# Attention products with V written three half-heads behind their scores, in a fused attention and mixer kernel

## The chip, the cores and the metric

The kernel runs on one core of one Trainium2 chip. The metric is the device time of one execution in microseconds, the median of several runs. Before the change it is 428.05 us, the median of 3 runs from 427.13 to 430.08.

## The reference, cut to what matters

Two batches of 12 heads, 448 tokens, head size 64: causal attention, then a mixer over tokens and channels, then a gated mixer. Only the attention part and what takes its output are touched by the change.

```python
scores = where(causal_mask, -1e9, q @ k.T / 8)
attn   = exp(scores - rowmax(scores)); attn = attn / (rowsum(attn) + 1e-9)
x      = attn @ v                                   # batch 2, heads 12, 448 x 64
h      = relu(x.T @ w_tok1) @ w_tok2;  u = x + h.T  # mix over tokens
y      = u + relu(u @ w_ch1) @ w_ch2                # mix over channels
# then gelu(y @ w_in), layer norm, a product over tokens, gate, w_out, residual
```

## The kernel before, in words

Heads are taken in **pairs** (12 pairs over both batches), and each head in two **halves**, so there are 48 half-heads. A half takes two of the four blocks of query rows (`HALVES`, `KW`), so that every half has 512 columns of scores at most. For one half-head, `probabilities` (lines 268 to 305) does this:

- TensorE: scores `s_ps` from q and k in f32 (line 286), into one of 2 PSUM buffers.
- VectorE: mask and row minimum into `pe` (line 291; 5 buffers, and 2 of their own for the first half of a second head).
- ScalarE: the bias (296), the exponential (298), the f16 high part `hl` (300; 4 buffers).
- GpSimd: the f16 low part of `hl` (301).
- SP: a transposing DMA from `hl` to `pT` (303; `pT` has 4 buffers).

`values` (316 to 328) then multiplies the transposed probabilities with V: three f16 products for each block of keys (lines 326, 327, 328). A pair has 60 of them, 20 on each line, and 18 records of score matmuls on line 286; over the 12 pairs that is 720 and 216. They gather in `x_ps`, of which there is one PSUM buffer, so that the first product of a pair waits until the pair before has been normalised out of it (342 to 344).

`prep_v` (248) loads V of one pair, finds its largest value, and splits it into f16 parts `vh` and `vl`, of which there are two sets that alternate by pair. `prep_qk` (239) loads q and k. `prepare` calls `prep_qk` four heads ahead and `prepare_v` calls `prep_v` two heads ahead; the latter stands in `tc.high_priority(offset=-80)`, which moves its instructions back in the order by 80 places. `load_tok` (233) brings in the weights of the token mix, each through ScalarE, VectorE and GpSimd. After every fourth head `token_mix` (356) multiplies the normalised `xh`, `xl` into `a_ps` and `u_ps`. `channel_up` (170) for seven of the column blocks of batch 0 can run beside attention: its weight loads stand in SP's queue behind the transposes of given heads (`issue_after(marks[...])`).

**What sets the order.** The program text is not the order in the queues. A planner runs the program against its own estimates of durations and gives each engine, at each moment, the instruction that is ready by these estimates (operands done, buffer free) and was written first. The result is a fixed queue for each engine, and on the chip each engine takes its queue in that order. Writing an instruction later therefore only means that others win against it when both are ready.

Of the kernel before, what the change touches and what calls it, by code (L numbers as in the profile page):

```python
# [11 lines left out]
F32 = mybir.dt.float32  # L12
# [15 lines left out]
def mixer_kernel(  # L28
# [20 lines left out]
    H, D = 2 * H2, D2 // 2  # L49
# [3 lines left out]
    P = 128  # L53
# [3 lines left out]
    GH = 4  # L57
# [1 line left out]
    WC = 768  # L59
    NF0 = 7  # L60
    AHEAD = 4
    VAHEAD = 2

    def f32(ap):
        return ap.bitcast(F32)
# [130 lines left out]
    with ExitStack() as at:  # L196
# [7 lines left out]
        ps_x = at.enter_context(tc.tile_pool(name="ps_x", bufs=1, space=PSUM))  # L204
# [28 lines left out]
        def load_tok():  # L233
            for c in range(NQ):
                load64(w1h[:, c, :], w1l[:, c, :], w_tok1[tok(c), :], "pool", twice=c == 0)
            for c in range(NT):
                load64(w2h[:, c, :], w2l[:, c, :], w_tok2[c * P:(c + 1) * P, :], "pool")
# [10 lines left out]
        def prep_v(b, n):  # L248

            vr = qkp.tile([P, NVC, 2 * D], F32, tag="vr", name="vr", bufs=2)  # L250
            nc.sync.dma_start(vr, v[b, n])
            hi, lo = vts[n % NVT]
            vr4 = vr.rearrange("p c (h d) -> p c h d", h=2)
            am = stp.tile([P, 1], BF16, tag="am", name="am")
            nc.vector.tensor_reduce(am, vr[:, 1:5], AX.XY, ALU.max, apply_absolute_value=True)
            pm = ps_e.tile([P, 512], F32, tag="d", name="vm")
            nc.tensor.matmul(pm[:, :P], am.to_broadcast([P, P]), ident_b, start=True, stop=True)
            sv = stp.tile([P, 1], F32, tag="sv", name="sv")
            nc.vector.reduce_max(sv, pm[:, :P], axis=AX.X)
            nc.vector.tensor_scalar(sv, sv, 1e-20, 1.0 / VSCALE, ALU.max, ALU.mult)  # L260
            nc.vector.reciprocal(sv, sv)
            nc.scalar.activation(hi[:, :, :, :D], vr4, AF.Copy, scale=sv[:, 0:1])
            nc.vector.scalar_tensor_tensor(lo, vr4, sv[:, 0:1], hi[:, :, :, :D], ALU.mult, ALU.subtract)
            return hi, lo, sv

        count = [0]

        def probabilities(qp, k2, hd, half):

            ps = ps_s.tile([P, NP], F32, tag="s", name="s_ps")
            if (hd, half) == (1, 0):
                pe, mx = pes[count[0] % len(pes)], mxs[count[0] % len(pes)]
            else:
                pe = xp.tile([P, NP], F32, tag="pe", name="pe", bufs=NPE)
                mx = stp.tile([P, 2], F32, tag="mx", name="mx")
            todo, o = [], 0
            for j, i in enumerate(HALVES[half]):
                w = KW[i]  # L280
                if i > 0 or hd == 0:
                    todo.append((j, i, slice(o, o + w)))
                    q0 = S - 64 if i == 0 else S + w - P if hd else w - P - 64
                    for ks in KEYS[i]:
                        m = ks.stop - ks.start
                        nc.tensor.matmul(ps[:, o:o + m], qp[:, q0:q0 + P], k2[:, ks], start=True, stop=True)  # L286
                        o += m
                else:
                    o += w
            for j, i, cs in todo:  # L290
                nc.vector.tensor_tensor_reduce(  # L291
                    out=pe[:, cs], in0=ps[:, cs], in1=mask0 if i == 0 else mask[:, MASKS[i]],
                    scale=-1.0 / math.sqrt(D), scalar=3.0e38, op0=ALU.add, op1=ALU.min, accum_out=mx[:, j:j + 1],
                )
            bias = stp.tile([P, 2], F32, tag="bias", name="bias")
            nc.scalar.add(bias, mx, math.log(PSCALE))
            for j, i, cs in todo:
                nc.scalar.activation(pe[:, cs], pe[:, cs], AF.Exp, bias=bias[:, j:j + 1], scale=-1.0)  # L298
            hl = hlp.tile([P, 2, NP], F16, tag="hl", name="hl", bufs=4)
            nc.scalar.copy(hl[:, 0], pe)  # L300
            nc.gpsimd.tensor_sub(hl[:, 1], pe, hl[:, 0])  # L301
            pT = hlp.tile([P, 2, NP // P, P], F16, tag="pT", name="pT", bufs=4)
            last[0] = nc.sync.dma_start_transpose(
                out=pT.rearrange("p a c q -> p (a c) q"), in_=hl.rearrange("p a n -> p (a n)")
            ).ins
            return pT
# [9 lines left out]
        def values(px, pT, hd, half, vh, vl):  # L316


            for i in HALVES[half]:
                for h in range(2) if i == 0 and hd == 0 else [hd] if i else []:  # L320
                    n = 64 if i == 0 else P
                    qs = slice(h * 64, h * 64 + 64) if i == 0 else slice(0, P)
                    o = px[qs, 2 * i - 1 + h if i else 0]
                    for j, (blk, c) in enumerate(MEET[i]):
                        ph, pl = pT[:, 0, blk, qs], pT[:, 1, blk, qs]
                        nc.tensor.matmul(o, ph, vh[:, c, h, :D + 1], start=j == 0, stop=False)  # L326
                        nc.tensor.matmul(o[:, :D], ph, vl[:, c, h, :], start=False, stop=False, skip_group_check=True)
                        nc.tensor.matmul(o, pl, vh[:, c, h, :D + 1], start=False, stop=j == i)

        def pair(b, e, qk, vs, x):  # L330

            (vh, vl, sv), (xf, xh, xl) = vs, x
            px = ps_x.tile([P, 7, D + 1], F32, tag="x", name="x_ps")
            for hd in range(2):
                for half in range(2):
                    pT = probabilities(*qk, hd, half)
                    values(px, pT, hd, half, vh, vl)
                if hd == 0:
                    yield
            count[0] += 1  # L340
            rd = stp.tile([P, 7, 1], F32, tag="rd", name="rd")
            nc.vector.tensor_scalar(rd, px[:, :, D:D + 1], 1e-9 * PSCALE, sv[:, 0:1], ALU.add, ALU.mult)
            nc.vector.reciprocal(rd, rd)
            nc.vector.tensor_mul(xf[:, e], px[:, :, :D], rd.to_broadcast([P, 7, D]))
            cs = slice(e * P, (e + 1) * P)
            x6 = xf[:, e, 1:].rearrange("p (c h) d -> p c (h d)", h=2)
            nc.scalar.copy(xh[:, 1:, cs], x6)
            sub(xl[:, :, cs], x6, xh[:, 1:, cs])

            for h in range(2):  # L350
                hs, ls = (slice(64 * i, 64 * i + 64) for i in (h, 1 - h))
                ds = slice(e * P + h * D, e * P + h * D + D)
                nc.gpsimd.tensor_scalar(xh[hs, 0, ds], xf[hs, e, 0], 1.0, 0.0, ALU.mult, ALU.add)
                sub(xh[ls, 0, ds], xf[hs, e, 0], xh[hs, 0, ds])
# [37 lines left out]
        last, marks = [None], []  # L392
        order = [(b, h) for b in range(B) for h in range(H)]
        qks, vss = {}, {}

        def prepare(n):
            if n < len(order):
                b, h = order[n]
                if h % 2 == 0:
                    qks[b, h // 2] = prep_qk(b, h // 2)  # L400

        def prepare_v(n):
            if n < len(order) and n % 2 == 0:
                b, h = order[n]

                with tc.high_priority(offset=-80):
                    vss[b, h // 2] = prep_v(b, h // 2)
# [3 lines left out]
        def up():  # L411

            m = dense.pop(0)
            with tc.issue_after(marks[H - 2 + m]):
                channel_up(m, [0], rpool, ps_e)

        for n in range(AHEAD):
            prepare(n)
        for n in range(VAHEAD):
            prepare_v(n)  # L420
        for n, (b, h) in enumerate(order):
            prepare(n + AHEAD)
            prepare_v(n + VAHEAD)
            if n == GH - 1:
                load_tok()
            if h % GH == 0:
                x = (
                    xp.tile([P, GH // 2, 7, D], F32, tag="xf", name="xf", bufs=2),
                    xp.tile([P, NQ, GH * D], F32R, tag="xh", name="xh"),
                    xp.tile([P, NQ - 1, GH * D], F32R, tag="xl", name="xl"),  # L430
                )
            if h % 2 == 0:
                it = pair(b, h % GH // 2, qks[b, h // 2], vss[b, h // 2], x)
            next(it, None)
            marks.append(last[0])
            if h % GH == GH - 1:
                token_mix(b, h // GH, *x)

            if (b, h) == (1, H - 2):
                up()  # L440

        while dense:
            up()
# [175 lines left out]
```

## Time and profile before

| what | value |
|---|---|
| median of 3 runs | 428.05 us (427.13 to 430.08) |
| the profiled execution | 429.13 us, span 427.3 us from its first to its last instruction |
| mean granted TensorE clock | 0.988 of full |
| busy share of the span | PE 94%, PEld 80%, POOL 58%, DVE 56%, ACT 48% |
| scores run | 4.6 to 141.7 us |
| products with V run | 18.4 to 154.3 us |

PE is TensorE's matmuls, PEld its weight loads, DVE VectorE, ACT ScalarE, POOL GpSimd, SPq the queue of SP, which issues the DMAs. A row of a table by stretches gives, for each engine, busy us and in brackets the number of its instructions, then the mean granted clock, the mean busy share of the 16 DMA engines and what they moved. A row of a timeline gives start, duration, engine, line, operation, tiles, the count of merged instructions, and in square brackets how long the engine sat idle before and what released it.

### The profile page before, as it was taken

The page shows a single profiled execution, that of the slowest core. Times are in us where ns is not written, and L with a number is a line of the kernel's source. Part 1 is how long each engine was busy: PE and PEld are TensorE (multiplying, and loading weights), DVE is VectorE, ACT ScalarE, POOL GpSimd, SP SyncE. Part 2 cuts the span into 40 slices and gives each one's busy share as a digit, 9 for nine tenths or more (in the row PEclk, how much of TensorE's full clock was granted, in tenths as well). Part 3 has the DMA queues.
Part 4 walks back from the last instruction along what each step waited for, and adds up shares of the span by engine and source line. Part 5 has one row for each costly group of instructions (what it writes and reads, how often), then busy time and mean ns, then how long its engine had stood idle before and what let it go on. Part 6 is the DMA issues. An engine that isn't in the chain of part 4 may idle for free.

```text
span 427.3 us, 6998 instructions
## 1 busy us (share of the span) xinstructions
PE 399.9 (94%) x2567; PEld 340.3 (80%) x2567; DVE 238.4 (56%) x522; ACT 204.2 (48%) x389; POOL 246.5 (58%) x234
## 2 busy tenths in 40 slices
PE   5878788888998999999999999999999999999996
PEld 3545666776787998999999999999998889965995
DVE  5989566787693645344444275557437451249422
ACT  3888678697665454445344244334423232332100
POOL 2789768769777564464335247454556653225662
PEclk9989999999898999999999999999999999999999
DMA  7999999999987854446344344453354001100122
GB/s 213 199 290 235 209 173 208 252 220 265 242 170 164 163 160 154 137 156 220 123 132 157 106 127 144 134 181 110 126 163 135 0 0 51 49 2 0 76 98 86
DMA packets 66738, 62.29 MB, mean 146 GB/s; under 512 B 53136, under 2 KB 58384, under 8 KB 66704
## 3 DMA queue, kind: packets, MB, share of 16 engines
q1 hardware_dynamic: 66704, 61.85, 56.5%
q8 instruction: 20, 0.33, 0.3%
q14 instruction: 14, 0.11, 0.1%
HBM read 46.50 MB, written 2.75 MB: 115 GB/s over the span
## 4 chain that ended last, share of the span: by engine, by line
PE 67%; DMA 12%; POOL 8%; ACT 5%; SPq 2%; issue 2%; DVE 2%; POOLq 0%; ACTq 0%; DVEq 0%
DMA pT<-hl 8%; PE y_ps L137 7%; PE y_ps L136 7%; PE y_ps L138 7%; PE r_ps L138 6%; PE r_ps L136 6%; PE r_ps L137 6%; POOL hl L301 4%; DMA vr<-in 2%; PE v_ps L138 2%; PE o_ps L136 2%; PE o_ps L138 2%; PE o_ps L137 2%; PE ug_ps L136 2%; PE v_ps L137 2%; PE ug_ps L138 2%
## 5 line engine op out<-in xcount | busy, mean ns | idle before, releaser
L94 POOL TENSOR_TENSOR wlo<-wm,whi 128x768 fp32r<-128x768 f32 (+1 forms) x41 | 81.3, 1984 | 75.6 <-ACT whi L121 75.1
L116 DVE TENSOR_SCALAR wm<-wm 128x768 int32<-128x768 int32 (+2 forms) x53 | 34.1, 643 | 88.0 <-ACT wm L113 88.0
L301 POOL TENSOR_TENSOR hl<-pe,hl 128x512 f16<-128x512 f32 x48 | 60.5, 1267 | 29.2 <-ACT hl L300 25.2
L113 ACT ACTIVATE wm<-wraw 128x768 f32<-128x768 f32 (+2 forms) x53 | 42.7, 805 | 59.1 <-POOL wlo L94 47.7
L286 PE MATMUL s_ps<-k,q 128*128 128x64 f32 (+3 forms) x216 | 57.9, 410 | 8.3 <-DMA q<-in 4.6
L138 PE MATMUL r_ps<-u_hi,wlo 128*128 128x448 f32 x144 | 53.4, 370 | 0.0
L137 PE MATMUL r_ps<-u_lo,whi 128*128 128x448 f32 x144 | 53.2, 369 | 0.0
L136 PE MATMUL r_ps<-u_hi,whi 128*128 128x448 f32 x144 | 53.1, 369 | 0.0
L136 PE MATMUL y_ps<-rh,whi 128*128 128x448 f32 x144 | 52.6, 365 | 0.0
L138 PE MATMUL y_ps<-rh,wlo 128*128 128x448 f32 x144 | 52.6, 365 | 0.0
L137 PE MATMUL y_ps<-rl,whi 128*128 128x448 f32 x144 | 52.6, 365 | 0.0
L121 ACT CAST whi<-wm 128x768 fp32r<-128x768 f32 (+1 forms) x41 | 32.8, 800 | 37.8 <-PE ug_ps L137 11.6
L117 DVE SCALAR_TENSOR_TENSOR wm<-wraw,wm 128x768 int32<-128x768 int32 (+2 forms) x53 | 50.1, 945 | 1.0
L286 PEld LDWEIGHTS s_ps<-k,q 128*128 128x128 f32 x216 | 32.4, 208 | 17.2 <-issue 6.6
L298 ACT ACTIVATE pe<-pe,bias 128x192 f32<-128x192 f32 (+3 forms) x84 | 40.2, 522 | 0.4
L291 DVE CUSTOM_DVE_ANT_0 pe<-s_ps,mask 128x320 f32<-128x320 f32 (+3 forms) x84 | 34.6, 444 | 7.9 <-PE s_ps L286 6.1
L300 ACT CAST hl<-pe 128x512 f16<-128x512 f32 x48 | 29.3, 612 | 18.3 <-DMA pT<-hl 17.9
L326 PE MATMUL x_ps<-vh,pT 128*128 128x65 f16 (+1 forms) x240 | 26.3, 197 | 11.6 <-DMA pT<-hl 10.9
L326 PEld LDWEIGHTS <-pT 128*128 128x128 f16 (+1 forms) x240 | 21.2, 98 | 19.6 <-DMA pT<-hl 14.6
L94 POOL TENSOR_TENSOR u_lo<-yt,u_hi 128x448 fp32r<-128x448 f32 x12 | 13.9, 1156 | 30.1 <-ACT u_hi L193 30.1
L138 PEld LDWEIGHTS r_ps<-u_hi,wlo 128*128 128x128 f32 x144 | 27.2, 189 | 2.6 <-issue 0.4
L136 PEld LDWEIGHTS r_ps<-u_hi,whi 128*128 128x128 f32 x144 | 27.3, 189 | 2.4 <-issue 0.2
(140 smaller groups left out, 918.7 us busy)
## 6 DMA issues: line engine op xcount, KB each, us to landing
wraw<-in SPq DMA_DIRECT2D x35, 768.0 KB, 4.5
wraw<-in SPq DMA_DIRECT2D x14, 512.0 KB, 3.9
vr<-in SPq DMA_DIRECT2D x12, 320.0 KB, 3.8
k<-in SPq DMA_DIRECT2D x12, 224.0 KB, 3.4
q<-in SPq DMA_DIRECT2D x24, 112.0 KB, 3.4
out<-ob SPq DMA_DIRECT2D x12, 224.0 KB, 1.9
wraw<-in SPq DMA_DIRECT2D x3, 256.0 KB, 3.1
pT<-hl SPq DMA_TRANSPOSE x48, 4.4
```

The lines of the kernel that those rows point to most:

```text
L94: nc.gpsimd.tensor_sub(lo, src, f32(hi))
L113: nc.scalar.activation(m, words.bitcast(F32)[:, :, 1], AF.Prelu, scale=2.0 ** -112, alpha=-(2.0 ** 32))
L116: nc.vector.tensor_scalar(mi, mi, 3, None, ALU.logical_shift_left)
L117: nc.vector.scalar_tensor_tensor(mi, words[:, :, 0], 29, mi, ALU.logical_shift_right, ALU.bitwise_or)
L136: nc.tensor.matmul(ps, lh, rh, start=i == 0 and not begun, stop=False)
L137: nc.tensor.matmul(ps, lh, rl, start=False, stop=False)
L138: nc.tensor.matmul(ps, ll, rh, start=False, stop=i == n - 1)
L286: nc.tensor.matmul(ps[:, o:o + m], qp[:, q0:q0 + P], k2[:, ks], start=True, stop=True)
L291: nc.vector.tensor_tensor_reduce(out=pe[:, cs], in0=ps[:, cs], in1=mask0 if i == 0 else mask[:, MASKS[i]], scale=-1.0 / math.sqrt(D), scal ...
L298: nc.scalar.activation(pe[:, cs], pe[:, cs], AF.Exp, bias=bias[:, j:j + 1], scale=-1.0)
L301: nc.gpsimd.tensor_sub(hl[:, 1], pe, hl[:, 0])
L326: nc.tensor.matmul(o, ph, vh[:, c, h, :D + 1], start=j == 0, stop=False)
```

## The change

Each half-head's `probabilities` is put on a list, and `products()`, which does the `values` of the oldest entry, is called once the list holds more than `LAG = 3`. So the products of a half-head are written behind the scores, exponentials and transposes of the three half-heads that follow it, also across heads and pairs. The normalisation of a pair, the next V preparation and the token mix move with the products. V of the first pair is prepared right behind q and k of the first pair and without the offset of 80; V of a later pair is prepared behind the normalisation of the pair two before it. No arithmetic, tile size or buffer count changes.

```diff
-    VAHEAD = 2
+    LAG = 3
...
-        def pair(b, e, qk, vs, x):
-
-            (vh, vl, sv), (xf, xh, xl) = vs, x
-            px = ps_x.tile([P, 7, D + 1], F32, tag="x", name="x_ps")
-            for hd in range(2):
-                for half in range(2):
-                    pT = probabilities(*qk, hd, half)
-                    values(px, pT, hd, half, vh, vl)
-                if hd == 0:
-                    yield
-            count[0] += 1
+        def normalise(px, e, sv, x):
+            xf, xh, xl = x
             rd = stp.tile([P, 7, 1], F32, tag="rd", name="rd")
...
         def prepare_v(n):
-            if n < len(order) and n % 2 == 0:
+            if n < len(order):
                 b, h = order[n]
                 with tc.high_priority(offset=-80):
                     vss[b, h // 2] = prep_v(b, h // 2)
...
-        for n in range(AHEAD):
-            prepare(n)
-        for n in range(VAHEAD):
-            prepare_v(n)
-        for n, (b, h) in enumerate(order):
-            prepare(n + AHEAD)
-            prepare_v(n + VAHEAD)
+        waiting = []
+        px = x = None
+        def products():
+            nonlocal px, x
+            b, h, half, pT = waiting.pop(0)
+            vh, vl, sv = vss[b, h // 2]
+            if (h % 2, half) == (0, 0):
+                px = ps_x.tile([P, 7, D + 1], F32, tag="x", name="x_ps")
+            values(px, pT, h % 2, half, vh, vl)
+            if (h % 2, half) != (1, 1):
+                return
...
+            normalise(px, h % GH // 2, sv, x)
+            prepare_v(b * H + h + 3)
+            if h % GH == GH - 1:
+                token_mix(b, h // GH, *x)
+
+        prepare(0)
+        vss[0, 0] = prep_v(0, 0)
+        for n in range(1, AHEAD):
+            prepare(n)
+        prepare_v(2)
+        for n, (b, h) in enumerate(order):
+            prepare(n + AHEAD)
             if n == GH - 1:
                 load_tok()
...
-            if h % 2 == 0:
-                it = pair(b, h % GH // 2, qks[b, h // 2], vss[b, h // 2], x)
-            next(it, None)
+            for half in range(2):
+                waiting.append((b, h, half, probabilities(*qks[b, h // 2], h % 2, half)))
+                if len(waiting) > LAG:
+                    products()
+            count[0] += h % 2
             marks.append(last[0])
-            if h % GH == GH - 1:
-                token_mix(b, h // GH, *x)
             if (b, h) == (1, H - 2):
                 up()
+        while waiting:
+            products()
         while dense:
             up()
```

## Rows read from the trace of the kernel before

**Rows 1.** By stretches: length; PE, PEld, DVE, ACT, POOL busy; clock, DMA, GB/s.

```profile
0.00:140.00 140.00, 116.84 (x1119) 90.02 (x1120) 100.93 (x313) 102.11 (x233) 104.58 (x128) 0.96 1.00 217
140.00:170.00 30.00, 29.31 (x213) 26.51 (x213) 16.04 (x30) 15.49 (x26) 17.05 (x16) 1.00 0.63 166
...
180.00:420.00 240.00, 240.00 (x1172) 211.44 (x1171) 116.77 (x173) 82.92 (x125) 120.31 (x88) 1.00 0.33 105
...
20.00:50.00 30.00, 22.99 (x264) 16.57 (x265) 25.26 (x82) 24.39 (x62) 27.04 (x32) 0.94 1.12 246
...
200.00:220.00 20.00, 20.00 (x101) 18.53 (x100) 8.79 (x14) 8.98 (x14) 8.68 (x5) 1.00 0.49 149
```

**Rows 2.** The chain that ended last, by engine and by line.

```profile
PE 67%; DMA 12%; POOL 8%; ACT 5%; SPq 2%; issue 2%; DVE 2%; POOLq 0%; ACTq 0%; DVEq 0%
```

**Rows 3.** Waits of the engines: us in total, times, longest.

```profile
ACT hl L300 <- DMA pT<-hl: 17.9, 11, 4.6
...
PE x_ps L326 <- DMA pT<-hl: 10.9, 11, 2.3
...
DVE am L255 <- DMA vr<-in: 9.7, 8, 3.5
```

**Rows 4.** Instructions of tile pT: DMA to landing.

```profile
DMA to landing us min/median/max: 3.0/4.4/7.3
```

**Rows 5.** By stretches, the score matmuls of line 286 alone.

```profile
0.00:26.70 26.70, 15.84 (x54) 9.14 (x54) 1.00 0.91 215
...
0.00:80.20 80.20, 41.09 (x150) 23.12 (x150) 0.98 1.04 216
```

**Rows 6.** By stretches, the products with V of line 326 alone.

```profile
0.00:26.70 26.70, 2.40 (x20) 1.82 (x20) 1.00 0.91 215
...
0.00:80.20 80.20, 13.40 (x120) 10.72 (x120) 0.98 1.04 216
```

**Rows 7.** By stretches, the low parts on GpSimd (line 301) alone.

```profile
0.00:80.20 80.20, 38.27 (x31) 0.98 1.04 216
```

**Rows 8.** Timeline of GpSimd around the first and the sixth pair's normalisation.

```profile
24.81 0.56 POOL L353 TENSOR_SCALAR xh<-xf 64x64 fp32r<-64x64 f32 x2 [0.78 <-DVE xf L344]
...
26.13 1.16 POOL L301 TENSOR_TENSOR hl<-pe,hl 128x512 f16<-128x512 f32 x1
...
82.04 1.15 POOL L353 TENSOR_SCALAR xh<-xf 64x64 fp32r<-64x64 f32 x4
```

**Rows 9.** Timelines of the start: SP, DVE, ACT and PE.

```profile
3.02 1.10 SPq L245 DMA_DIRECT2D q<-in  x2
...
5.94 1.06 SPq L251 DMA_DIRECT2D vr<-in  x2
...
10.92 1.35 SPq L303 DMA_TRANSPOSE pT<-hl  x1
...
10.03 0.69 DVE L255 TENSOR_REDUCE am<-vr 128x1 bf16<-128x512 f32 x1 [0.48 <-DMA vr<-in]
...
18.20 1.10 DVE L263 SCALAR_TENSOR_TENSOR vl<-vr,sv,vh 128x640 f16<-128x640 f32 x1
...
17.30 1.53 ACT L262 ACTIVATE vh<-vr,sv 128x640 f16<-128x640 f32 x2
...
11.45 1.19 PE L286 MATMUL s_ps<-k,q 128*128 128x64 f32 x4
...
18.38 0.22 PE L326 MATMUL x_ps<-vh,pT 128*64 128x65 f16 x1
```

**Rows 10.** Waits of SP's queue: us in total, times, longest.

```profile
SPq L303 <- PE x_ps L328: 8.3, 6, 5.0
```

**Rows 11.** Timelines around 75 to 90 us: GpSimd and SP.

```profile
74.84 2.28 POOL L301 TENSOR_TENSOR hl<-pe,hl 128x512 f16<-128x512 f32 x2 [0.16 <-ACT hl L300]
...
81.10 2.06 SPq L303 DMA_TRANSPOSE pT<-hl  x1
...
90.21 2.27 POOL L301 TENSOR_TENSOR hl<-pe,hl 128x512 f16<-128x512 f32 x2 [3.33 <-ACT bias L296]
```

More of the change, by code (lines that the diff above doesn't have):

```diff
@@ L415, in up @@
                 channel_up(m, [0], rpool, ps_e)
-        for n in range(AHEAD):
-            prepare(n)
-        for n in range(VAHEAD):
-            prepare_v(n)
-        for n, (b, h) in enumerate(order):
-            prepare(n + AHEAD)
-            prepare_v(n + VAHEAD)
-            if n == GH - 1:
-                load_tok()
-            if h % GH == 0:
+        waiting = []
[9 more added lines that the diff above has]
+                return
+            if h % GH == 1:
                 x = (
@@ L431, in mixer_kernel @@
                 )
-            if h % 2 == 0:
-                it = pair(b, h % GH // 2, qks[b, h // 2], vss[b, h // 2], x)
-            next(it, None)
-            marks.append(last[0])
+            normalise(px, h % GH // 2, sv, x)
+            prepare_v(b * H + h + 3)
             if h % GH == GH - 1:
                 token_mix(b, h // GH, *x)
+        prepare(0)
[5 more added lines that the diff above has]
+            prepare(n + AHEAD)
+            if n == GH - 1:
+                load_tok()
+            for half in range(2):
[3 more added lines that the diff above has]
+            count[0] += h % 2
+            marks.append(last[0])
             if (b, h) == (1, H - 2):
                 up()
+        while waiting:
+            products()
         while dense:
```

## The prediction

> **What bounds the kernel now.** I read the table by stretches first [rows 1]. The span falls into two parts. From 180 to 420 us PE is busy 240.00 of 240 us: nothing the change touches lies there, and none of it can be won. Up to 170 us, attention, nothing is full: to 140 us PE is busy 116.84 of 140 us, POOL 104.58, ACT 102.11, DVE 100.93. From 140 to 170 us PE is again at 29.31 of 30, since the channel matmuls of batch 0 fill it. So a gain must come out of PE's idle time before 140 us, 140 - 116.84 = 23.2 us. Of this 4.6 us are the first load of q and k, which stays. **The ceiling is 18.6 us.**
>
> Then the chain [rows 2]: PE 67%, DMA 12%, POOL 8%, ACT 5%; in attention it jumps from engine to engine. The waits [rows 3] say why: a product with V waits on PE for its transpose 11 times, 10.9 us, and ACT waits for a transpose to give an `hl` buffer back 11 times, 17.9 us. A transpose lands 4.4 us (3.0 to 7.3) after its issue [rows 4]. Last, the stretch from 20 to 50 us, where POOL is busy 27.04 of 30 us and DVE and ACT 25 and 24 [rows 1]: there PE, at 22.99, waits for the elementwise engines.
>
> **Part 1: products three half-heads behind their scores.** The question is whether the queues don't have this order already. A pair has 18 score records and 20 records of line 326, so 4.5 and 5 per half-head. Up to 26.70 us PE ran 54 score records, 54 / 4.5 = 12 half-heads [rows 5], and 20 of line 326, 20 / 5 = 4 half-heads [rows 6]. The fifth half-head's products stand behind the scores of the twelfth: seven behind their own. Up to 80.20 us it is 150 records, 144 for 32 half-heads and 6 that complete the 33rd and begin the 34th, against 120 / 5 = 24: the 25th's products stand eight behind. **The planner already runs scores further ahead than LAG asks**, as far as the buffers let it. Rule "scores of the next three first" is met; and against scores four or more ahead the products win in both texts. I cost this at 0 us. What covers it is the depth of the buffers (2 score tiles, 5 `pe`, 4 `hl`, 4 `pT`), which is unchanged; were the queues only as deep as the text, the 10.9 us of waits would be in play.
>
> **Part 2: normalisation and token mix move with the products.** 12 normalisations on DVE, ACT and POOL and 6 token mixes, no instruction more. They now lose against the low parts, casts and masks of three more half-heads. Up to 80.20 us POOL had done 31 low parts [rows 7]; when it normalises there, at 82.04 [rows 8], the new order wants 4 x 6 + 3 = 27 done before the sixth pair. So that order stands too. At the first pair it doesn't: the normalisation at 24.81 goes ahead of the low part at 26.13 [rows 8], and its two pieces (0.56 us) would go behind it. One low part 0.6 to 1.3 us earlier, an `xh` as much later: 0 us in the sum.
>
> **Part 3: V preparation.** Still 12 times, same instructions, same two buffers. Before, V of a pair is written 4 half-heads of products ahead of its first use (at the start of the pair before); after, behind the normalisation of the pair two before, so again 4. The offset of 80 stays. DVE waits for V loads 8 times, 9.7 us [rows 3], with the masks queued behind it. As the 12 loads pass other transposes and q, k loads in SP's queue, this could vanish or double: from -9.7 to +9.7 us of DVE, which has 25.26 busy in 30 us where it is tightest; I take 0, as the distance is the same.
>
> **Part 4: first V first.** This is the one sure change. The first V's issue leaves 5.94 us and goes behind the first q: about 3 us earlier; the later q and k issues slip by one issue, 1.06 / 2 = 0.53 us [rows 9]. The second pair's first scores start at 11.45 us, and its q is issued by 4.1 us, so with the transposes' median of 4.4 us as a stand-in it lands by 8.5 + 0.5 us: hidden, with over 2 us to spare. What it gives: one of the two ScalarE splits of V that stand together at 17.30 us (1.53 us) moves out of the crowded stretch into ACT's idle time, 1.53 / 2 = 0.8 us; on DVE the maximum (0.69) and low part (1.10) move likewise [rows 9]. The first product, at 18.38, could follow its transpose (issued at 10.92, 1.35 to issue, 4.4 to land: 16.7 at the latest) some 1.7 us sooner, but no transpose waits for that. POOL, the tightest engine from 20 to 50 us, gets nothing off its back. Between 0 and 1.8 us I take ACT's **0.8 us**, because casts stand right behind those splits.
>
> **Part 5: a new plan.** Small differences early shift every later choice of the planner, which no row shows. Bounds from the nearest rows: at best it takes out all of PE's waits for transposes, -10.9 us [rows 3]; at worst it doubles what SP's transposes wait for products to free `pT`, 8.3 us in 6 waits [rows 10]. I take 0 between them, and keep both for the range.
>
> **Sum.** 0 + 0 + 0 - 0.8 + 0 = -0.8 us. The profiled execution took 429.13 us, so 428.3 for a like one; it stands 1.1 us above the median of 428.05, from which the same sum gives **427 us**.
>
> How full is PE really in attention? Per instruction its busy time overlaps the next one's. Weight loads are busy 18.53 of 20 us where PE never stops, and 90.02 + 26.51 = 116.5 us in the first 170 [rows 1]. The Trainium skill, "Perfetto Trace Analysis", section "Identifying the Most-Contended Engine", holds that matmul busy share is a poor measure of headroom and weight-load busy share a better one. By it attention needs 116.5 x 20 / 18.53 = 125.8 us of PE, and an ideal order would win 165.4 - 125.8 = 39.6 us where busy time leaves 19.3 (to 170 us); the trace cannot bear that out, since POOL, ACT and DVE are all busy over 100 of the first 140 us.
>
> **The rivals.**
>
> *Faster: the new plan frees PE of the transposes.* If products reach PE only when their transposes have landed, 10.9 us of waits go: 427.2 - 10.9 = 416 us, 422 for half of it. For it: the waits are real and the planner sees transposes as quicker than they land, or it would not have put products in front of them. Against: the distance is seven or eight half-heads already, and next in line POOL binds from 20 to 50 us (3 us of slack there). Chance of a gain over 1%: 0.34.
>
> *Slower: the ring of transposes.* With LAG 3 exactly four `pT` are written ahead of the oldest product, and there are four buffers. If a product comes on PE later than the next transpose has its data, that transpose waits, SP's queue behind it too (loads of q, k, V, weights), then `hl`, then ACT's cast with the exponentials behind it, then POOL. It has happened before: low parts done from about 76 us [rows 11], their transpose issued at 81.10, the following low part at 90.21 after 3.33 us of POOL idle. It decides when products start later than the low part four half-heads on. Twice the present 8.3 us: 427.2 + 8.3 = 435.5 us. Chance of a loss over 1%: 0.24.
>
> *Not what it says* is the forecast itself: the lag changes no order on PE. Chance of within 1%: 0.42.
>
> **How the numbers follow.** About 1% (4.3 us) is what a measurement of this kernel can tell from no change: under 423.8 us counts as faster, over 432.3 as slower. The likeliest case, 427 us, has its own range from 423.8 to 432. With 0.34 and 0.24 outside it, the range for 8 in 10 must go into both rivals: down to 416.5, where nearly all 10.9 us are won, and up to 436, where the ring costs its 8.3.
>
> **What would show it.** Right: in the profile after, score records ahead of the products at 27 and 80 us stay within one or two half-heads of seven and eight; PE's waits for transposes stay near 11 us; the first product starts near 16 us; PE busy to 140 us stays near 117. Wrong to the fast side: waits of PE on `pT` under 5 us, and the last product well before 154 us. Wrong to the slow side: SP's transposes waiting for products over 16 us, or ACT's cast waiting for transposes over 25 us. The forecast fails if the lag in the queues has become much smaller or larger than before, since then the text does set the order.

## The result, and the profile after

The changed kernel takes **431.41 us** in the median of 20 runs (429.96 to 433.50). The kernel before, run between them 20 times, takes 428.74 us. The ratio of the paired runs is **1.0083, with a 95% interval of 1.0060 to 1.0105**: slower by 0.8%, where 427 us, a gain of 0.8 us, was forecast. The time lies inside the range given (416.5 to 436). The profiled execution took 431.45 us, span 429.7 us, at a mean granted clock of 0.984. Before it was 427.3 us and 0.988, so the profiled spans differ by 2.4 us.

Table by stretches of the kernel after (columns as in [rows 1]):

```profile
0.00:140.00 140.00, 116.65 (x1117) 88.64 (x1118) 102.73 (x310) 101.21 (x230) 101.26 (x126) 0.95 0.99 214
140.00:170.00 30.00, 28.59 (x201) 25.11 (x200) 19.71 (x29) 16.41 (x28) 20.68 (x18) 1.00 0.55 161
20.00:50.00 30.00, 21.68 (x184) 14.36 (x181) 21.85 (x67) 22.01 (x55) 26.58 (x32) 0.80 1.06 215
180.00:420.00 240.00, 240.00 (x1171) 211.44 (x1170) 118.22 (x174) 81.99 (x126) 120.77 (x88) 1.00 0.33 105
...
0.00:180.00 180.00, 155.24 (x1369) 123.08 (x1370) 126.78 (x346) 122.47 (x264) 124.07 (x146) 0.96 0.88 201
```

The last of these rows in the kernel before:

```profile
0.00:180.00 180.00, 156.15 (x1380) 125.80 (x1381) 120.34 (x347) 121.26 (x265) 125.84 (x146) 0.97 0.90 202
```

To 140 us PE's busy time is what it was: 116.65 us against 116.84 [rows 1]. It is the stretch from 20 to 50 us that differs most: PE 21.68 against 22.99 at a clock of 0.80 against 0.94, with POOL still the fullest engine (26.58 against 27.04). From 180 to 420 us PE is full in both. Over the first 180 us, PE is idle 180 - 155.24 = 24.8 us (before 23.8). The clock's cost I estimate as the span times the missing share of the clock, which treats every microsecond as PE's: 429.7 x (1 - 0.984) = 6.9 us (before 427.3 x 0.012 = 5.1). **1.0 us of idle and 1.8 us of clock** are 2.8 us, against the 2.4 us by which the spans differ. This says where the time shows, and not yet what caused it.

The chain that ended last, by engine, of the kernel after, to be held against [rows 2]:

```profile
PE 67%; DMA 11%; POOL 8%; DVE 5%; issue 4%; SPq 3%; ACT 2%; POOLq 0%; ACTq 0%; DVEq 0%
```

DVE has 5% in place of 2%, ACT 2% in place of 5%: the chain now passes more through VectorE and less through ScalarE. The waits of the kernel after, to be held against [rows 3] and [rows 10] (us in total, times, longest):

```profile
ACT wm L113 <- DMA wraw<-in: 17.8, 12, 2.7
DVE am L255 <- DMA vr<-in: 13.2, 8, 5.1
ACT hl L300 <- DMA pT<-hl: 13.0, 12, 4.2
PE x_ps L326 <- DMA pT<-hl: 6.7, 10, 1.6
...
PE x_ps L326 <- DVE xf L337: 2.9, 2, 2.5
...
SPq L303 <- POOL hl L301: 31.2, 21, 5.6
...
SPq L303 <- PE x_ps L328: 4.4, 2, 4.0
```

Three of these waits in the kernel before:

```profile
ACT wm L113 <- DMA wraw<-in: 6.6, 5, 2.0
...
PE x_ps L326 <- DVE xf L344: 0.6, 2, 0.4
...
SPq L303 <- POOL hl L301: 18.7, 18, 2.0
```

The waits on which the forecast's rivals stood all shrank: ACT for a transpose from 17.9 to 13.0 us, PE for one from 10.9 to 6.7, SP for products from 8.3 to 4.4. The kernel is slower all the same. What grew: V's load waits (9.7 to 13.2), ACT's waits for weights to load (6.6 to 17.8), SP's waits for GpSimd's low parts, without which no transpose can be issued (18.7 to 31.2), and PE waiting for VectorE to normalise a pair out of `x_ps` (0.6 to 2.9, of which 2.5 us at one stroke).

**The start.** DVE after, then POOL after (start, us, engine, line, what):

```profile
11.68 0.69 DVE L255 TENSOR_REDUCE am<-vr 128x1 bf16<-128x512 f32 x1 [1.90 <-DMA vr<-in]
12.28 0.61 DVE L291 CUSTOM_DVE_ANT_0 pe<-s_ps,mask 128x448 f32<-128x448 f32 x1
```

```profile
15.53 0.40 POOL L119 TENSOR_SCALAR w1h<-wm 128x256 fp32r<-128x256 f32 x1 [0.70 <-DVE wm L117]
16.02 0.73 POOL L94 TENSOR_TENSOR w1l<-wm,w1h 128x256 fp32r<-128x256 f32 x1
18.01 0.97 POOL L119 TENSOR_SCALAR w1h<-wm 128x256 fp32r<-128x256 f32 x1 [1.26 <-DVE wm L117]
18.95 1.15 POOL L301 TENSOR_TENSOR hl<-pe,hl 128x512 f16<-128x512 f32 x1
```

The mask of the third half-head on DVE, and its low part, the third, on POOL, in the kernel before:

```profile
10.63 0.61 DVE L291 CUSTOM_DVE_ANT_0 pe<-s_ps,mask 128x448 f32<-128x448 f32 x1
...
15.11 1.16 POOL L301 TENSOR_TENSOR hl<-pe,hl 128x512 f16<-128x512 f32 x1 [0.34 <-ACT hl L300]
```

With the first V early, the planner put the second V's maximum on DVE in front of the mask of the third half-head. DVE waited 1.90 us there for the load, the mask started at 12.28 (before at 10.63), and in POOL's queue three pieces of token weights came ahead of the third low part, which started at 18.95 in place of 15.11. The transposes of the third and fourth half-heads were issued at 20.1 and 22.5 us (before 16.7 and 18.1). The delay stays for most of attention: the 20th transpose is issued at 65.1 us (before 60.0) and the 32nd at 96.0 (88.8). By the 41st it is gone (121.8 against 124.6), and the last is issued at 148.4 (147.6).

**The stall near 40 us.** PE, then DVE, of the kernel after:

```profile
38.03 0.19 PE L328 MATMUL x_ps<-vh,pT 128*128 128x65 f16 x1
40.74 0.23 PE L326 MATMUL x_ps<-vh,pT 128*64 128x65 f16 x2 [2.52 <-DVE xf L337]
```

```profile
35.57 1.02 DVE L263 SCALAR_TENSOR_TENSOR vl<-vr,sv,vh 128x640 f16<-128x640 f32 x1
36.51 1.49 DVE L116 TENSOR_SCALAR wm<-wm 128x512 int32<-128x512 int32 x1
38.04 1.53 DVE L117 SCALAR_TENSOR_TENSOR wm<-wraw,wm 128x512 int32<-128x512 int32 x1
39.49 0.21 DVE L335 TENSOR_SCALAR rd<-x_ps,sv 128x7 f32<-128x7 f32 x1
39.74 0.20 DVE L336 RECIPROCAL rd<-rd 128x7 f32<-128x7 f32 x1
39.97 0.62 DVE L337 TENSOR_TENSOR xf<-x_ps,rd 128x448 f32<-128x448 f32 x1
```

The products of a pair end at 38.2 us, and there is one `x_ps`. The normalisation that frees it stands on DVE behind a V low part and two pieces of token weights, in sum 4 us without a gap, so PE's queue stops for 2.52 us. The stretches around it in the kernel after:

```profile
34.00:38.00 4.00, 4.00 (x52) 2.73 (x51) 3.13 (x6) 3.81 (x11) 3.91 (x5) 0.92 1.16 195
38.00:41.00 3.00, 0.48 (x15) 0.35 (x12) 2.90 (x6) 2.85 (x7) 3.00 (x3) 1.00 1.06 271
41.00:44.00 3.00, 2.42 (x17) 0.91 (x15) 1.59 (x9) 1.74 (x5) 2.84 (x5) 0.58 1.01 241
44.00:48.00 4.00, 1.78 (x20) 1.60 (x20) 2.98 (x10) 1.09 (x5) 3.79 (x6) 0.50 1.36 151
48.00:52.00 4.00, 4.00 (x26) 2.60 (x26) 0.85 (x5) 2.65 (x6) 2.96 (x3) 0.54 0.61 151
52.00:56.00 4.00, 4.00 (x44) 3.79 (x40) 3.43 (x12) 2.92 (x7) 1.53 (x1) 1.00 0.56 142
```

After a stretch in which PE was busy 0.48 of 3 us, the granted clock falls to 0.50 (1.2 GHz), and it is back at 1.00 (2.4 GHz) from 52 us on. The groups of instructions by line and shape, of 44 to 51.5 us and of 52 to 75 us, have the same score matmul at both levels (count, busy us, mean ns):

```profile
L286 PE MATMUL s_ps<-k,q 128*128 128x448 f32 x2 | 1.8, 1008 | 0.0
...
L286 PE MATMUL s_ps<-k,q 128*128 128x448 f32 x8 | 3.9, 573 | 0.0
```

It takes 1008 ns in place of 573. A stall of 2.5 us was followed by some 10 us at the low clock, in which such a matmul took that much longer.

### The profile page after: what moved, and what is told of

It is laid out like the page before. It is cut to its first block, busy times and chain, and to the rows that moved or that the text cites. A ratio compares the mean times of both kernels' runs of the same rounds, so it can differ in the third digit from the quotient of the medians.

```text
span 429.7 us, 7000 instructions
## 1 busy us (share of the span) xinstructions
PE 401.4 (93%) x2567; PEld 339.8 (79%) x2567; DVE 246.9 (57%) x522; ACT 204.5 (48%) x389; POOL 246.2 (57%) x234
## 4 chain that ended last, share of the span: by engine, by line
PE 67%; DMA 11%; POOL 8%; DVE 5%; issue 4%; SPq 3%; ACT 2%; POOLq 0%; ACTq 0%; DVEq 0%
PE y_ps L137 7%; PE y_ps L136 7%; PE y_ps L138 7%; PE r_ps L137 5%; PE r_ps L138 5%; PE r_ps L136 5%; DMA vr<-in 5%; DMA pT<-hl 4%; POOL hl L301 3%; DMA wraw<-in 3%; PE v_ps L136 2%; PE o_ps L138 2%; PE o_ps L136 2%; PE o_ps L137 2%; PE v_ps L138 2%
## 5 line engine op out<-in xcount | busy, mean ns | idle before, releaser
L116 DVE TENSOR_SCALAR wm<-wm 128x768 int32<-128x768 int32 (+2 forms) x53 | 35.0, 661 | 93.1 <-ACT wm L113 93.1
L301 POOL TENSOR_TENSOR hl<-pe,hl 128x512 f16<-128x512 f32 x48 | 59.4, 1246 | 32.1 <-ACT hl L300 26.6
L286 PE MATMUL s_ps<-k,q 128*128 128x64 f32 (+3 forms) x216 | 59.7, 418 | 7.7 <-DMA q<-in 4.6
L117 DVE SCALAR_TENSOR_TENSOR wm<-wraw,wm 128x768 int32<-128x768 int32 (+2 forms) x53 | 62.8, 1186 | 1.1
L291 DVE CUSTOM_DVE_ANT_0 pe<-s_ps,mask 128x192 f32<-128x192 f32 (+3 forms) x84 | 34.6, 444 | 8.3 <-PE s_ps L286 8.1
L326 PE MATMUL x_ps<-vh,pT 128*128 128x65 f16 (+1 forms) x240 | 27.6, 200 | 11.3 <-DMA pT<-hl 6.7
L94 POOL TENSOR_TENSOR u_lo<-yt,u_hi 128x448 fp32r<-128x448 f32 x12 | 15.8, 1313 | 30.3 <-ACT u_hi L193 30.3
```

The source lines that it names most:

```text
L94: nc.gpsimd.tensor_sub(lo, src, f32(hi))
L116: nc.vector.tensor_scalar(mi, mi, 3, None, ALU.logical_shift_left)
L117: nc.vector.scalar_tensor_tensor(mi, words[:, :, 0], 29, mi, ALU.logical_shift_right, ALU.bitwise_or)
L291: nc.vector.tensor_tensor_reduce(out=pe[:, cs], in0=ps[:, cs], in1=mask0 if i == 0 else mask[:, MASKS[i]], scale=-1.0 / math.sqrt(D), scal ...
```

## The experiments

Theories. **T1, the parts:** the lag or the V order costs what is seen, each by its own wait. **T2, the start:** the late third transpose is the cost. **T3, late V:** written behind the products, the V preparations of later pairs come too late. **T4, the plan:** any new order of the queues moves the time by about as much, and the change drew a bad one. In the expectations, START is T2, RE-PLAN is T4, and LAG is the lag's share of T1. A "plan" is the set of queues that the planner made of one text. Each kernel has 6 to 12 timed runs beside 20 to 35 of the kernel before on the same chip. A result is the ratio to the kernel before, with its 95% interval. "Old start" is the load order of before (q and k of four heads, then V); "first V first" that of the change.

**The change in halves.** The kernel before with the first V alone moved:

```diff
-        for n in range(AHEAD):
-            prepare(n)
-        for n in range(VAHEAD):
-            prepare_v(n)
+        prepare(0)
+        vss[0, 0] = prep_v(0, 0)
+        for n in range(1, AHEAD):
+            prepare(n)
```

> The kernel before with one edit: V of the first pair prepared right behind q and k of the first pair, without the offset; no lag. Theory START (the loss is made in the first 35 us: after the change the fourth transpose is issued at 22.5 us instead of 18.1 us, because the maximum of the second V waits for its load in front of the masks): 431 to 432 us, fourth transpose at 22 us or later. Theory LAG (writing products behind three more half-heads costs): 428 to 429 us, fourth transpose still late but caught up. Theory RE-PLAN (any edit reshuffles all queues and moves the time by about 1% either way): anything from 424 to 435 us.

Measured: 1.0092 [1.0059, 1.0125].

The kernel after with the old start, so the lag alone:

```diff
-        prepare(0)
-        vss[0, 0] = prep_v(0, 0)
-        for n in range(1, AHEAD):
+        for n in range(AHEAD):
             prepare(n)
+        prepare_v(0)
+        prepare(AHEAD)
         prepare_v(2)
```

> The changed kernel with the loads at the start in the order of before (q and k of three pairs, then V of two pairs, both with the offset); LAG 3 stays. Theory START: 428 to 429 us, fourth transpose near 18 us. Theory LAG: 431 to 432 us. Theory RE-PLAN: 424 to 435 us, whatever the start does.

Measured: 1.0080 [1.0050, 1.0110]. PE's waits for transposes:

```profile
PE x_ps L326 <- DMA pT<-hl: 3.3, 6, 0.9
```

From 10.9 us [rows 3] down to 3.3, and slower: this wait isn't what sets the time.

The kernel after with `LAG = 0`:

> The changed kernel with LAG 0, so that products follow their own half-head in the text; first V first stays. Theory START: 431 to 432 us. Theory LAG: 428 to 429 us. Theory RE-PLAN: 424 to 435 us.

Measured: 1.0062 [1.0030, 1.0094].

With `LAG = 0` and the old start, so that only the later V preparations stand elsewhere in the text:

> The changed kernel with LAG 0 and with the loads at the start in the order of before: of the change only the place of the later V preparations (behind the normalisation) is left. Theories START and LAG: both 428 to 429 us, as before. Theory RE-PLAN: 424 to 435 us.

Measured: 0.9985 [0.9953, 1.0018]. Either half costs as much as both together (1.0092 and 1.0080 against 1.0083). Costs of two waits would add; T1 is in doubt.

**The start mended.** The second V's load is put behind the first transpose in SP's queue, first V still first, with LAG 0 and with LAG 3:

```diff
-        prepare_v(2)
...
                 waiting.append((b, h, half, probabilities(...)))
+                if (n, half) == (0, 0):
+                    with tc.issue_after(last[0]):
+                        prepare_v(2)
```

> LAG 0 and first V first, as the third experiment, but the load of the second V stands in SP's queue behind the first transpose, so that its maximum no longer stands on VectorE in front of the third half-head's mask. Theory START (that maximum is what first V first costs): the fourth transpose at 18 to 19 us instead of 22.3, and 426 to 428 us. Theory RE-PLAN (first V first costs nothing of its own, any new plan lands anywhere): the start is mended, the time is anywhere from 424 to 435 us, by chance still near 430.

> The changed kernel with the same mend of the start; LAG 3. Theory START with a cost of the lag of its own (0.8% in the second experiment): fourth transpose at 18 to 19 us, 429.5 to 431.5 us. Theory START alone (lag costs nothing): 426 to 428 us. Theory RE-PLAN: 424 to 435 us.

Measured: 1.0043 [1.0012, 1.0074] and 1.0104 [1.0056, 1.0152]. The mend does most of what it should; the third low part of the LAG 0 kernel on POOL:

```profile
15.06 1.17 POOL L301 TENSOR_TENSOR hl<-pe,hl 128x512 f16<-128x512 f32 x1
```

It starts as early as before the change (15.11). The third transposes are issued at 16.2 and 15.9 us (before 16.7), the fourth at 19.6 and 19.7 (before 18.1, with the change 22.5). The time hardly follows: 1.0062 to 1.0043 with LAG 0, 1.0083 to 1.0104 with LAG 3, inside each other's intervals. T2 falls as the whole cause.

**Neutral plans.** The kernel before, with one number changed that isn't part of the change, the number of places by which V preparations are moved back: 70, 76 or 60 in place of 80.

```diff
-                with tc.high_priority(offset=-80):
+                with tc.high_priority(offset=-70):
```

> The kernel before with the offset of the V preparations 70 instead of 80: no step of the change is in it, yet the planner's queues differ (1882 of PE's lines). Theory RE-PLAN: off by 0.5 to 1% from before, as likely as not slower. Theories START and LAG: within 0.4% of before, 427 to 429.5 us.

> The same with an offset of 76, which gives a third plan. Theory RE-PLAN: off by 0.5 to 1% from before, and not by the same as with 70. Theories START and LAG: within 0.4% of before, 427 to 429.5 us.

> The kernel before with one number changed: V preparation is moved back in the order by 60 places in place of 80. No lag, no new load order. A third neutral new plan beside the two tried (offset 70: 1.0084, offset 76: 0.9998). If a new plan alone moves the time by a per cent, this gives any value from 0.995 to 1.010; if the plan of before is no better than a typical one, the mean of the three stands near 1.000, and if it is a lucky one, near 1.005.

Measured: 1.0084 [1.0045, 1.0123], 0.9998 [0.9959, 1.0037] and 1.0074 [1.0041, 1.0107]. Two of three reorderings without any intent cost what the change costs. This is the first evidence for T4. All three turn the same knob, the place of the V preparations; a reordering that leaves V alone was not tried.

**Other lags, old start.** `LAG = 1` and `LAG = 2`:

> Change with V's load order of before at the start and LAG 1 in place of 3. If the written lag itself costs time (the V preparations of later pairs, written behind products, come later the larger the lag), the loss grows with the lag: LAG 0 measured 0.9985 of before, LAG 3 1.0080, so LAG 1 gives about 1.001 to 1.003 (427 to 428 us) and LAG 2 about 1.005. If only the luck of a new plan counts, the lags stand in no order: LAG 1 can be as slow as LAG 3 (1.006 or more), or LAG 2 faster than LAG 1.

> Same with LAG 2. By a cost of the lag itself: between LAG 1 and LAG 3, about 1.005 (429 us). By the luck of the plan: anything between 0.998 and 1.010, in no order with the lag.

Measured: 1.0068 [1.0031, 1.0105] and 0.9956 [0.9922, 0.9990]. With LAG 0 at 0.9985 and LAG 3 at 1.0080 there is no order in the lag.

**V prepared early, LAG 3, old start.** The V preparations of later pairs go back to where LAG 0 has them, which takes a third set of V buffers:

```diff
-        NPE, NVT = 5, 2
+        NPE, NVT = 5, 3
...
-            prepare_v(b * H + h + 3)
...
+            if h % 2:
+                prepare_v(n + 3)
             count[0] += h % 2
```

> LAG 3 and V's load order of before at the start, and a third set of V buffers, so that the V preparations of later pairs are placed where LAG 0 places them. If the later V loads are what LAG 3 loses by, it comes back to 427 us (ratio under 1.003), and DVE's maxima start as early as with LAG 0. If not, it stays at 430 to 431 us (1.006 to 1.010). The third set of buffers alone could also help by up to 2 us, which would put it below before.

Measured: 0.9967 [0.9940, 0.9993], against 1.0080 without the edit. Taken alone, this run would have passed for the proof of T3. So the same edit went into the changed kernel and into LAG 1, and a second plan (offset 70) was put under LAG 3 with the edit and without it:

> The changed kernel with a third set of V buffers and the V preparations of later pairs placed in the text where LAG 0 places them; first V still first, LAG 3. If the later V preparations are the cause of the loss with LAG 3, this falls from 1.008 to about 0.997 (the start with first V first may keep 0.002 to 0.004 of the loss, so up to 1.001). If e8 was a lucky plan, it stays anywhere from 0.998 to 1.010, and 1.006 or more refutes the late V preparation.

> LAG 1 with V's load order of before at the start, and the same third set of V buffers with V preparation placed as with LAG 0. By the late V preparation: from 1.0068 (LAG 1 without it) to about 0.997. By the luck of the plan: no relation to 1.0068; any value from 0.996 to 1.010.

> The LAG 3 kernel with the early V preparation (measured 0.9967), with the offset of V preparation 70 in place of 80: another plan of the same text. If 0.9967 is a property of the early V preparation, this stays between 0.994 and 1.000. If it was the luck of one plan, it moves by up to 0.01, as offset 70 moved the kernel before (1.0084).

> The LAG 3 kernel with the late V preparation and the old order at the start (measured 1.0080), with offset 70: another plan of the same text. If the late V preparation costs what it did, this stays at 1.005 to 1.010. If 1.0080 was the luck of one plan, it can come out at 0.996 to 1.002.

Measured: 1.0038 [1.0008, 1.0067]; **1.0127** [1.0079, 1.0174]; 0.9958 [0.9925, 0.9992]; **0.9951** [0.9913, 0.9989]. With the edit against without: 1.0080 to 0.9967, 1.0083 to 1.0038, 1.0068 to 1.0127, 0.9951 to 0.9958. Two down, one up, one unmoved: T3 falls. And LAG 3 with late V, 1.0080 under one plan, is 0.9951 under another, with intervals far apart: the value belongs to the plan and not to the lag. The kernel before had 1.0084 with offset 70, so the lag with late V cost 0.0080 under offset 80 and won 0.0133 under offset 70.

**The changed kernel in other plans.** Offset 70 and 60 in it:

> The changed kernel with one number changed: V preparations of later pairs moved back by 70 places in place of 80, which gives another plan of the same change. If the change itself costs 0.8%, this stays at 1.005 to 1.011 (429.5 to 432 us). If its loss was that of one plan among others, this can fall anywhere from 0.995 to 1.013; under 1.003 speaks for the plan.

> Same with 60 places, a third plan of the same change. By a cost of the change itself: 1.005 to 1.011 again. By the plan: 0.995 to 1.013, and not the same value as with 70 or 80.

Measured: 1.0088 [1.0047, 1.0128] and 1.0040 [1.0010, 1.0071]. Here T4's hope of a fast plan isn't met: three plans of the change are all slower, by 0.4 to 0.9%.

**All of them together.** Clock is the mean granted clock over the timed runs.

| start | kernel | ratio | clock |
|---|---|---|---|
| old | before | 1 | 0.990 |
| old | LAG 0 | 0.9985 | 0.991 |
| old | before, offsets 70 / 76 / 60 | 1.0084 / 0.9998 / 1.0074 | 0.985 / 0.990 / 0.986 |
| old | LAG 1 / 2 / 3 | 1.0068 / 0.9956 / 1.0080 | 0.983 / 0.992 / 0.987 |
| old | LAG 3, offset 70 | 0.9951 | 0.987 |
| old | early V: LAG 1 / LAG 3 / LAG 3, offset 70 | 1.0127 / 0.9967 / 0.9958 | 0.978 / 0.992 / 0.994 |
| first V first | after, offsets 80 / 70 / 60 | 1.0083 / 1.0088 / 1.0040 | 0.984 / 0.986 / 0.985 |
| first V first | before with it / LAG 0 | 1.0092 / 1.0062 | 0.980 / 0.981 |
| first V first | mended: LAG 0 / LAG 3 | 1.0043 / 1.0104 | 0.988 / 0.983 |
| first V first | after, early V | 1.0038 | 0.989 |

The 11 plans with the old start other than before have a mean of 1.0023 with a standard deviation of 0.0064 (2.7 us); the eight with first V first 1.0069 and 0.0026, none under 1.0038. The difference of the means, 0.0046, is two of its standard errors (0.0022, from the root of 0.0064 x 0.0064 / 11 + 0.0026 x 0.0026 / 8). The runs allow a sharper comparison: five pairs of kernels that differ in the start alone (old start, then first V first). "32nd" is when the 32nd transpose is issued, and "PE" is PE's busy time in the first 20 us, both from one profile each:

| the rest of the kernel | ratio | 32nd, us | PE, us |
|---|---|---|---|
| before | 1 / 1.0092 | 88.8 / 95.4 | 14.22 / 11.90 |
| LAG 0 | 0.9985 / 1.0062 | 90.2 / 95.2 | 13.42 / 12.92 |
| LAG 3 | 1.0080 / 1.0083 | 92.2 / 96.0 | 13.52 / 12.96 |
| LAG 3, offset 70 | 0.9951 / 1.0088 | 90.0 / 93.0 | 13.10 / 12.54 |
| LAG 3, early V | 0.9967 / 1.0038 | 90.2 / 93.6 | 14.02 / 12.37 |

First V first is slower in all five, with the intervals apart in four. The mean difference is 0.0076, or 3.3 us, with a standard error of 0.0022. In all five PE has done less by 20 us (at a clock of 1.00), and the 32nd transpose comes 3.0 to 6.6 us later. So first V first most likely has a cost of its own. The pairs were not set up as a test of it, and in the plan of the change itself the difference is 0.0003: there the lag with late V had lost as much already.

**What a plan's time consists of.** For 19 of these profiles (all but that of offset 70 in the kernel before, whose profiled execution lay 0.7% over its median) I took PE's idle time to 180 us (180 minus its busy time) and the clock's cost over the span (span times 1 minus the mean clock). The span less both is 397.7 us with a standard deviation of 1.2 (395.6 to 399.1), while the spans themselves go from 422.9 to 431.5. Their sum follows the span with a correlation of 0.93, idle alone with 0.60. This is close to bookkeeping: a span is PE's idle time, its work at full clock and what a lower clock adds. It tells in which of the two a plan loses, and not why. The extremes, LAG 3 with early V (span 422.9 us, clock 0.996) and LAG 1 with early V (431.5 us, 0.975):

```profile
0.00:180.00 180.00, 156.82 (x1402) 128.12 (x1403) 125.67 (x353) 122.61 (x268) 129.91 (x147) 0.99 0.88 206
```

```profile
0.00:180.00 180.00, 154.91 (x1360) 126.63 (x1361) 119.98 (x347) 119.56 (x262) 124.85 (x145) 0.94 0.85 201
```

Idle 23.2 against 25.1 us, clock 422.9 x 0.004 = 1.7 against 431.5 x 0.025 = 10.8 us. Of 8.6 us of span, 1.9 are idle and 9.1 clock (the sum is 2.4 us over, twice the 1.2). Over the timed runs it is the same: the ratios of the 20 kernels and their mean clocks correlate at -0.85. But the clock isn't fixed by the plan: one run of LAG 3 with offset 70 took 421.27 us at 0.996 and another 427.56 at 0.979, and that kernel is the fastest of all with a mean clock (0.987) under that of before (0.990).

## Why the prediction was wrong

**Part 4, "the one sure change", failed in its sign.** It priced each moved instruction by where it had stood, -0.8 us, and assumed that everything else on the queue stayed. It didn't: the second V's maximum came in front of a mask, DVE waited 1.90 us for the load, and the third low part came 3.8 us later. The first product did start sooner, at 17.1 us against 18.4 (about 16 forecast), and nothing was won by it. What the runs show in place of a gain of 0.8 us is a loss of 0.1 to 5.9 us in five pairs, 3.3 in the mean. By which wait isn't shown: the mended start issues its third transpose in time, yet its two kernels are at 1.0043 and 1.0104, against 0.9985 and 1.0080 with the old start.

**Part 5 failed, by its size.** "Small differences early shift every later choice of the planner ... I take 0 between them." A new plan moved this kernel by -0.5 to +1.3% (-2.1 to +5.4 us), inside the bounds of -10.9 and +8.3 us. A spread of 2.7 us, that of the plans with the old start, is three times the gain that the sum forecast, so the sum could not tell the sign. Whether 0 was also the wrong centre is open: 13 of 19 new plans are slower than before, but eight of those have first V first, and of the 11 others five are slower and six not. The three neutral plans have a mean of 1.0052, which hints that the plan of before was a good draw. The loss of the change, 0.8%, is of the size of two neutral reorderings (0.8 and 0.7%), and of the mean of the five pairs; how it divides between the two isn't shown.

**Part 2, "0 us in the sum", left out that `x_ps` has one buffer.** It followed the normalisation on POOL, where it does little, and not on DVE, where PE waits for it. That wait went from 0.6 us to 2.9, and the clock fell after it. It is 3.5 us in the changed kernel with offset 70 and 0.9 with offset 60, whose ratio is the lower one, 1.0040. But it is 3.1 us in the changed kernel with early V (1.0038), and 0.8 and 0.9 in the two kernels with first V first and no lag (1.0092 and 1.0062), so it is at most one way of losing among several.

**The sum had no term for the clock.** It took PE's idle time, 23.2 us, as all that could be won. [rows 1] had a clock of 0.96 in the same 140 us, 140 x 0.04 = 5.6 us more by the same estimate, and that is where the larger part of the difference shows: 1.8 us of 2.8 between the two profiles; over the timed runs 428 x (0.990 - 0.984) = 2.6 of the 3.6 us of the ratio.

**Part 1 was right in its count.** The score records done at the same counts of products, in the kernel after (columns as in [rows 5]):

```profile
0.00:27.00 27.00, 17.17 (x60) 9.79 (x61) 1.00 0.84 200
0.00:80.20 80.20, 40.73 (x138) 22.24 (x138) 0.91 0.94 199
```

With 20 and 120 records of line 326 at these times, as in [rows 6], 60 / 4.5 = 13 and 138 / 4.5 = 31 half-heads stand against the fifth's and the 25th's products: eight and six ahead, where seven and eight had been. The lag asked for three, the queues ran at more than that with and without it, and its value, 0 to 3, shows no order in the times. Of its signs, PE's waits for transposes staying near 11 us did not hold (6.7). **Part 3**: the V load waits moved by +3.5 us, inside its ±9.7; placing V early again moved the time either way.

**The range held by luck.** Its slow end was the ring of transposes, which did not come (4.4 us where 16.6 were feared); the loss of 3.6 us came without it and merely fits inside.

**The rivals.** *Slower, the ring of transposes*, fell: its mark was over 16 us of SP waiting for products, and it is 4.4. The loss came without it. *Faster*: half of its mechanism happened (10.9 to 6.7 us of PE's waits, 3.3 with the lag alone), and nothing came of it, because PE then waited for other engines: its idle time as a whole rose by 1.0 us. The Trainium skill, "Perfetto Trace Analysis", section "Identifying the Most-Contended Engine", takes the busy share of the weight loads as one measure of TensorE's headroom. The estimate by it was 39.6 us; the fastest of the plans tried won 2.1, so no run here bears it out.

**A version that beats both.** LAG 3 with the old start and offset 70 is at 0.9951 [0.9913, 0.9989] of before, LAG 2 with the old start at 0.9956 [0.9922, 0.9990]: some 2 us under before, 5 to 6 under the change. They are chosen from 20, so that a part of their lead may be chance, and both keep the old start.

**Open** is by which wait first V first costs its 3 us, as the mended start shows that it isn't the late third transpose alone, and why the lag, with late V, loses under one plan and wins under another.

## What to carry to other kernels

Where a planner orders the queues, any edit draws a new plan: measure how far a few neutral edits move the time before a half per cent is put down to the edit, and repeat an experiment that "proves" a cause under other plans: an edit that moves the time the same way in all of them, as first V first did, most likely has an effect of its own; one that changes its sign, as the lag did, has shown none. In forecasting such an edit, compare the kernel's present plan with a few neutral ones first, and give the range at least their spread. A wait that shrinks is no gain where the engine is held by several others in turn: add up the engine's whole idle time, and the cost of its clock.

## What was not expected of the hardware

The granted clock was where the larger part of the differences between plans of the same work showed: by the estimate above from 1.7 to 10.8 us of the span, at 0.50 (1.2 GHz) in pieces that lie nearly all in attention. In the kernel after, the longest piece follows the stretch in which PE was busy 0.48 of 3 us, and the same score matmul then took 1008 ns in place of 573. Such a stall can cost twice: once as idle time, and once more in the work that comes after it. The one does not measure the other: in the changed kernel with offset 70 the wait for `x_ps` was longer, 3.55 us, and the clock was 0.90 from 40 to 44 us, 0.67 from 44 to 48, and 1.00 from 48 to 60.
